# Windowed attention into a gated MLP on one core: stores of weight sums held until the last weight is decoded, and the product of a head pair issued together with the scores two pairs on

## The chip, the cores and the metric

The kernel runs on 1 core of one Trainium2 chip. The metric is the time of one execution in device microseconds (us). Before the change the median of 3 runs is 877.01 us (874.94 to 877.79).

## The reference

What is computed, cut to what matters: masked attention for 8 batches x 8 heads of 576 positions and 64 channels, and then a two-layer MLP on the 4608 tokens of 512 channels.

```python
scores = q @ k.T / sqrt(64)                       # per batch and head, 576 x 576
mask_plain = (rel >= 0) & (rel < 32)              # heads 0 to 3, rel = query - key
mask_dil = (rel >= 0) & (rel < 128) & (rel % 4 == 0)      # heads 4 to 7
attn = softmax(where(mask, scores, -1e9))
x = (attn @ v) -> [4608, 512]
h = x @ w_in                                      # w_in 512 x 2048
g = h * (1 / (1 + exp(-1.702 * h)))
out = g @ w_out                                   # w_out 2048 x 512, all float32
```

## The kernel before, in words

**Attention.** The work is cut into 32 entries `k`, each a pair of heads of one batch: batch `b = k // 4`, four entries a batch (`NC` is 4). For each entry TensorE makes `scores(k)` (L429, 72 small matmuls with q and k as 64 x 32 and 64 x 64 operands, into the tile `sp`); VectorE, ScalarE and GpSimd make the softmax (`softmax`, which starts with `exponentials`); the weights are transposed and copied into the one tile `bt`; TensorE makes `product(k)` (L537, 36 matmuls of 96 x 64, 32 of them into the tile `av` and 4 into a spare strip of an `sp` tile); ScalarE and VectorE take the result out (`drain_x`). For entries 0 to 7 (`masked`) the mask is added by a matmul; from entry 8 on VectorE adds it while it takes the scores out of `sp` (`add_mask`). For entries 4 to 7 the copies into `bt` are DMAs (L496), later they are done by ScalarE and VectorE. There is one buffer each of q/k (`qk`), v (`v`), `bt`, `av` and `sp`, and two each of the softmax tiles, taken by turns.

**The order of an entry's steps** is written in `attention(k)`. Before, `scores(k + 1)` is its own step on TensorE, issued by `alone(k + 1)`, and `product(k)` is another, which comes later.

**MLP.** Batches 0 to 2 go through groups `m0` to `m2` (`Group`): for each of 16 slices `f` of the hidden width, 12 matmuls into the one bank `hp_m` (L769), ScalarE's tanh (L777), VectorE's gating (L778), which frees `hp_m`, a split into a high and a low part (`gh`, `gl`), and then 12 matmuls into the accumulators `acc_m` (L678, L679, L682). Batches 3 to 7 and the rest go through three blocks `p`, `q`, `r` (`Block`), which multiply sums of tokens with sums of weights (seven products for eight). The blocks read the sums from DRAM: `sum_weights(u)`, u from 0 to 7, writes three of seven sums as they stand in the weights (L794, three stores of 256 KB, so 24 in all), makes the other four on VectorE and GpSimd in arena areas 0 to 7, and writes these (L815, 1 MB). The down-weights of slices 9 to 15 are also copied to DRAM (L996, seven stores of 512 KB to `outs`), since the blocks overwrite their places.

**Decoding.** The float32 weights come as 32 chunks of 512 KB (`wi` and `wo` by turns, chunk 2f is w_in of slice f and chunk 2f + 1 is w_out of it). `decode(n)` fetches a chunk into one of five cells (L332) and splits it into a high and a low part with some six steps on ScalarE (L342, L343, L336), VectorE (L346 and others) and GpSimd. Slice f of group m0 can be made only when chunk 2f is decoded, and added to the accumulators only when chunk 2f + 1 is. So m0 runs beside the decoding, and m1 and all that follows runs after it.

**What sets the order.** Nothing is issued as the loops run. Each step is given to a planner (`Plan.add`) with its costs by engine, an urgency (smaller first), the names it reads and writes. `Plan.ordered` then goes through time by these costs, puts each step on the engine on which it would end first, and writes out one fixed order for each engine; a step's place is given by

```python
when, e = min((min(start(i, e) for i in mine[e]), e) for e in range(5) if mine[e])
here = [i for i in mine[e] if start(i, e) <= when]
i = min(here, key=lambda i: ops[i][1])
```

that is, of the steps that can start, the one with the smallest urgency. The urgencies that matter here: pieces of `hp` and `acc` 0, decoding `25 + 2.3 n`, attention of entries 8 to 11 `2000 + c`, `sum_weights` `2500 + 10 u`, the stores to `outs` 2600; scores and products have 100000 less than their entry. All DMAs spoken of here are issued by one queue, SP's, in the order so found. Engines take their instructions strictly in that order.

Of the kernel before, what the change touches and what calls it, by code (L numbers as in the profile page):

```python
# [17 lines left out]
P = 128  # L18
NC = DM // P
NF = DF // P  # L20
# [150 lines left out]
def tile_windowed_attention_then_gated_mlp(  # L171
# [27 lines left out]
    def bank(shape, tag, name):  # L199
        return ps.tile(shape, F32, tag=tag, name=name)  # L200
# [159 lines left out]
    def lots(k):  # L360

        if 0 < k < NC:
            return f"first qk{k}", f"first v{k}"
        return "qk0", "v0"
# [75 lines left out]
    def exponentials(k, urgency):  # L440
        u, y = pairs[k], k % 2
        pr, mx = prs[y], mxs[y]
        PR, MX = f"pr{y}", f"mx{y}"
        held = ("sp",) if masked(k) else ()

        def sp():
            return u["all"] if masked(k) else pr

        if FIRST * NC <= k < INNER:
            add_mask(k, urgency)  # L450
        add({DVE: 0.80}, urgency, lambda e: V.tensor_reduce(out=mx, in_=sp(), axis=AX.X, op=ALU.max),
            held or (PR,), (MX,))
        add({DVE: 0.80}, urgency, lambda e: pair(
            e, pr, sp(), mx[:, :, :, None].broadcast_to([P, 2, QT, W]), ALU.subtract), (*held, MX), (PR,))
        add({ACT: 0.75}, urgency, lambda e: A.activation(prs[y], prs[y], AF.Exp, scale=0.125), (), (PR,))
# [68 lines left out]
    def product(k):  # L524
        u = pairs[k]
        if k < INNER:
            u["av"] = bank([P, GT], "av", f"av_{k}")
            sp = pairs[k + 1]["sp"] if k + 1 < INNER else bank([P, 2, GT], "sp", f"rest_{k}")
            u["rest"] = sp[:, 1, QT * W:QT * W + LT]
        else:  # L530
            sp = bank([P, 2, GT], "sp", f"av_{k}")
            u["av"], u["rest"] = sp[:, 0], sp[:, 1, 0:LT]
        for m in range(NW):
            for a in range(2):
                rows = slice(D * a, D * a + D)
                dst = u["av"][rows, D * m:D * m + D] if m < NW - 1 else u["rest"][rows]
                T.matmul(dst, u["v"][a][0:KW, m], bt[0:KW, a, m], start=True, stop=True, skip_group_check=True)  # L537
# [77 lines left out]
    def attention(k, urgency):  # L615

        def alone(j):
            add({PE: 1.6 if masked(j) else 1.1}, urgency - 1.0e5, lambda e: scores(j),
                (lots(j)[0], *(["mask"] if dilated(j) else [])), ("sp", "left", f"scores{j}"), 1.0)
            if j >= INNER:  # L620
                add_mask(j, urgency)

        if k in (NC, INNER):
            load_qk(k)
            alone(k)
        load_v(k)
        more = k + 1 < len(pairs) and k + 1 != INNER
        if more:
            load_qk(k + 1)
        softmax(k, urgency)  # L630
        if more:
            alone(k + 1)
        add({PE: 1.25}, urgency - 1.0e5, lambda e: product(k),
            (lots(k)[1], *(f"bt.{m}" for m in range(8)), *([f"scores{k + 1}"] if more else [])),
            ("sp",) if k >= INNER else ("left", "av"), 1.0)
        drain_x(k, urgency)


    def unit(i):
# [147 lines left out]
    def sum_weights(u):  # L787


        f, g = u, u + PAIRS  # L790
        urgency = 2500.0 + 10.0 * u
        half = slice(0, 2 * P), slice(2 * P, 4 * P)
        for n, (w, cols) in enumerate(((f, half[0]), (f, half[1]), (g, half[1]))):
            add({DMA: 262}, urgency, lambda e, n=n, w=w, cols=cols: load(  # L794
                sums[7 * u + n].rearrange("p (h n) -> p h n", h=2), f32(wi(w)[:, :, cols])), (f"wi{w}",), (f"sums{u}.{n}",))
        b1, b2 = arena[:, 6], arena[:, 7]
        t = area(4, 2).rearrange("p (i n) -> p i n", i=4)
        parts_ = area(0, 4).rearrange("p (h i n) -> p h i n", h=2, i=4)

        def both(e, dst, w):  # L800
            pair(e, dst, f32(wi(w)[:, 0]), f32(wi(w)[:, 1]), ALU.add)

        add(add_costs, urgency, lambda e: both(e, b1, f), (f"wi{f}",), own(6))
        add(add_costs, urgency, lambda e: both(e, b2, g), (f"wi{g}",), own(7))
        keys = (*own(4), *own(5))
        for dst, x, y, costs in ((0, lambda: b2[:, half[0]], lambda: b1[:, half[0]], 0), (2, lambda: b2[:, half[1]], lambda: b2[:, half[0]], 0),
                                 (1, lambda: b2[:, half[1]], lambda: t[:, 0], 0), (3, lambda: b1[:, half[1]], lambda: t[:, 1], 0)):
            add({DVE: -0.40, POOL: 0.75}, urgency, lambda e, dst=dst, x=x, y=y: pair(e, t[:, dst], x(), y(), ALU.subtract),
                ("A6", "A7"), keys)
        places = [k for i in range(4) for k in own(i)]  # L810
        high = parts_[:, 0].bitcast(F32R)
        add({ACT: 1.05, DVE: -0.75}, urgency, lambda e: copy(e, high, t), ("A4", "A5"), places)
        add({DVE: -1.25, POOL: 2.6}, urgency, lambda e: pair(e, parts_[:, 1].bitcast(F32R), t, parts_[:, 0], ALU.subtract),
            ("A4", "A5", "A0", "A1"), ("A2", "A3"))
        add({DMA: 1049}, urgency, lambda e: load(  # L815
            sums[7 * u + 3:7 * u + 7].rearrange("i p (h n) -> p h i n", h=2), parts_), [f"A{i}" for i in range(4)], [f"sums{u}.{n}" for n in range(3, 7)])
# [165 lines left out]
    for b, g in enumerate(main):  # L982
        g.split_x()
        if b == 0:
            for n in range(2, 2 * NF - 8):
                decode(n, 25.0 + 2.3 * n)
            zeroed = [f"bt.{m}" for m in range(8)]
            add({POOL: 1.2}, 20.0, lambda e: G.memset(bt[0:KW], 0.0), (), ("bt", "btl", *zeroed))
            add({ACT: 0.5}, 30.0, lambda e: mask_dilated(), (), ("mask",))
        if b == 1:  # L990
            for c in range(NC):
                attention(2 * NC + c, 2000.0 + c)
            for u in range(PAIRS):
                sum_weights(u)
            for f in range(KEPT, NF):
                add({DMA: 524}, 2600.0, lambda e, f=f: load(outs[f].rearrange("p (h n) -> p h n", h=2), f32(wo(f))),  # L996
                    (f"wo{f}",), (f"outs{f}",))
        if b == 2:
            for k in range(3 * NC, INNER):
                attention(k, 1000.0 * (k // NC) + k % NC)  # L1000
        for f in range(NF):
            g.up(f)
            if b == 0 and f == 2:
                for c in range(NC):
                    attention(NC + c, 46.0 + 12.9 * c)
                for n in range(2 * NF - 8, 2 * NF):
                    decode(n, 25.0 + 2.3 * n)
# [74 lines left out]
```

## Time and profile before

| | |
|---|---|
| median of 3 runs | 877.01 us |
| the profiled execution's own time | 877.82 us |
| its span, first to last instruction | 876.1 us |
| TensorE matmuls busy | 853.5 us (97%) |
| VectorE, ScalarE, GpSimd busy | 521.6, 450.8, 148.8 us |
| mean granted TensorE clock | 0.992 |
| moved by DMA | 145.81 MB |

PE is TensorE's matmuls, PEld its loading of weights, which overlaps them, DVE is VectorE, ACT is ScalarE, POOL is GpSimd, SP the queue that issues the DMAs. A row of a timeline reads: start, length, engine, line, operation, tiles and count, and in brackets the idle time of the engine before it and what ended that. A matmul's record is longer than the time it holds TensorE, since matmuls are pipelined: a stream of 128 x 512 matmuls starts one every 0.227 us (12 of them fill 2.72 us) though each record has 0.39 us. The chain of waits is followed back from the last instruction: at each step to what released it.

### The profile page before, as it was taken

To read this page: it belongs to the slowest core of one execution; us is meant where nothing else is said; L and a number is where in the kernel's file an instruction comes from. 1 tells how busy PE (TensorE), PEld (TensorE's weight loads), DVE (VectorE), ACT (ScalarE), POOL (GpSimd) and SP (SyncE) were. 2 spreads that over 40 slices of the span, in tenths; PEclk is the share of its full clock that TensorE was granted. 3 is DMA by queue.
4 is the path that set the end of the run, shared out by engine and by line. 5 is a ranking of instruction groups with operands and counts; after the bars stand their busy time and mean duration, and the time that the engine had idled before them with its cause. 6 is when DMAs were issued, how large, how long until landed. Compare 5 with 4: busy or idle time off the path is not lost.

```text
span 876.1 us, 17851 instructions
## 1 busy us (share of the span) xinstructions
PE 853.5 (97%) x7160; PEld 688.8 (79%) x7160; DVE 521.6 (60%) x923; ACT 450.8 (51%) x789; POOL 148.8 (17%) x156
## 2 busy tenths in 40 slices
PE   6999989999999999999999999999999999999997
PEld 3677767878877877778788888888888888888786
DVE  6797877788577677777744544534346433434321
ACT  7897866656354555666753434433334343333322
POOL 3351414664111251021200100000001000000000
PEclk9799999999999999999999999999999999999999
DMA  9697884756364404977754631455456045543221
GB/s 351 188 348 225 248 296 161 221 177 196 108 207 151 130 29 122 325 227 241 232 176 128 215 99 48 146 151 168 124 142 220 1 136 143 153 145 108 48 73 49
DMA packets 89011, 145.81 MB, mean 166 GB/s; under 512 B 25952, under 2 KB 40544, under 8 KB 88928
## 3 DMA queue, kind: packets, MB, share of 16 engines
q1 hardware_dynamic: 88784, 144.54, 52.3%
q8 instruction: 57, 0.93, 0.4%
q14 instruction: 26, 0.21, 0.1%
q10 hardware_dynamic: 144, 0.13, 0.0%
HBM read 109.25 MB, written 34.08 MB: 164 GB/s over the span
## 4 chain that ended last, share of the span: by engine, by line
PE 88%; DMA 7%; DVE 2%; ACT 2%; issue 1%; SPq 0%; DVEq 0%; ACTq 0%
PE hp_m L769 13%; PE up_r L877 9%; PE up_p L877 8%; PE up_q L877 8%; PE acc_m L678 4%; PE acc_m L682 4%; PE acc_m L679 4%; PE av L537 3%; PE sp L429 3%; DMA qk<-qk_dram 2%; DMA arena<-wi_dram 2%; PE acc_pa L678 2%; PE acc_pa L682 2%; PE acc_rb L678 2%; PE acc_pa L679 2%; PE acc_rb L682 2%
## 5 line engine op out<-in xcount | busy, mean ns | idle before, releaser
L769 PE MATMUL hp_m<-xs,wi_kept 128*128 128x512 f32 x504 | 129.1, 399 | 4.1 <-DVE arena L778 3.6
L769 PEld LDWEIGHTS hp_m<-xs,wi_kept 128*128 128x128 f32 x504 | 93.6, 190 | 26.2 <-DVE arena L778 5.3
L297 DVE TENSOR_TENSOR gl<-arena,gh 128x512 fp32r<-128x512 f32 x108 | 78.8, 730 | 48.8 <-ACT gh L290 23.6
L290 ACT ACTIVATE gh<-arena 128x512 fp32r<-128x512 f32 x109 | 68.9, 632 | 56.3 <-DVE arena L909 15.8
L877 PE MATMUL up_p<-wi_kept,xs 128*128 128x512 f32 x336 | 86.8, 394 | 0.0
L877 PE MATMUL up_r<-wi_kept,xs 128*128 128x512 f32 x336 | 83.3, 390 | 0.0
L877 PE MATMUL up_q<-wi_kept,xs 128*128 128x512 f32 x336 | 83.3, 390 | 0.0
L297 POOL TENSOR_TENSOR pr<-pr,sm 128x320 f32<-128x320 f32 x64 | 51.7, 825 | 153.4 <-DVE sm L461 138.7
L908 ACT ACTIVATE arena<-arena 128x512 f32<-128x512 f32 x57 | 36.0, 632 | 80.3 <-DVE arena L297 80.2
L877 PEld LDWEIGHTS up_q<-wi_kept,xs 128*128 128x128 f32 x336 | 63.1, 188 | 13.0
L877 PEld LDWEIGHTS up_r<-wi_kept,xs 128*128 128x128 f32 x336 | 63.1, 188 | 13.0
L877 PEld LDWEIGHTS up_p<-wi_kept,xs 128*128 128x128 f32 x336 | 62.4, 188 | 13.4
L290 ACT ACTIVATE bt<-ct 32x320 f32<-32x320 f32 x125 | 58.7, 470 | 10.3 <-DVE ct L482 7.8
L678 PE MATMUL acc_m<-gh,wo_kept 128*128 128x512 f32 x156 | 62.5, 400 | 0.0
L679 PE MATMUL acc_m<-gh,wo_kept 128*128 128x512 f32 x156 | 60.9, 390 | 0.0
L909 DVE SCALAR_TENSOR_TENSOR arena<-arena 128x512 f32<-128x512 f32 x57 | 41.3, 724 | 25.1 <-ACT arena L908 25.0
L297 POOL TENSOR_TENSOR arena<-arena 128x256 f32<-128x256 f32 (+2 forms) x43 | 40.2, 947 | 57.4 <-DVE arena L297 24.4
L297 POOL TENSOR_TENSOR wi_kept<-arena,wi_kept 128x512 fp32r<-128x512 f32 x14 | 19.9, 1423 | 172.4 <-PE up_q L877 102.1
L777 ACT ACTIVATE arena<-hp_m 128x512 f32<-128x512 f32 x48 | 28.9, 601 | 34.2 <-PE hp_m L769 34.0
L778 DVE SCALAR_TENSOR_TENSOR arena<-arena,hp_m 128x512 f32<-128x512 f32 x48 | 32.9, 686 | 18.8 <-ACT arena L777 18.5
L682 PE MATMUL acc_m<-gl,wo_kept 128*128 128x512 f32 x156 | 42.5, 393 | 0.0
L297 DVE TENSOR_TENSOR arena<-up_q,arena 128x512 f32<-128x512 f32 x19 | 13.1, 689 | 49.2 <-PE up_q L877 49.1
(194 smaller groups left out, 1687.7 us busy)
## 6 DMA issues: line engine op xcount, KB each, us to landing
xs<-sums SPq DMA_DIRECT2D x168, 256.0 KB, 2.7
qk<-qk_dram SPq DMA_DIRECT2D x29, 576.0 KB, 5.0
v<-vp_dram SPq DMA_DIRECT2D x56, 216.0 KB, 3.0
wo_kept<-outs SPq DMA_DIRECT2D x18, 512.0 KB, 3.5
out_dram<-arena SPq DMA_DIRECT2D x35, 256.0 KB, 2.7
sums<-arena SPq DMA_DIRECT2D x8, 1024.0 KB, 5.6
arena<-wi_dram SPq DMA_DIRECT2D x15, 512.0 KB, 5.7
arena<-wo_dram SPq DMA_DIRECT2D x15, 512.0 KB, 6.3
```

The source lines that it names most:

```text
L290: A.activation(dst, src, AF.Copy, scale=scale)
L297: (V if e == DVE else G).tensor_tensor(out=dst, in0=a, in1=b, op=op)
L429: T.matmul(dst[:, w:w + n], u["qk"][rows, at:at + 32], u["qk"][rows, S + first:S + first + n], start=not masked(k), stop=True, tile_positi ...
L678: T.matmul(self.acc[j], w[:, 0, cols], high, start=f == self.order[0], stop=False)
L679: T.matmul(self.acc[j], w[:, 1, cols], high, start=False, stop=False)
L682: T.matmul(self.acc[j], w[:, 0, P * j:P * j + P], low, start=False, stop=f == self.order[-1])
L769: T.matmul(hps[f], wi(f)[:, st, cols], mv[:, c], start=c == 0 and k == 0, stop=c == NC - 1 and k == 2)
L777: add({ACT: 0.60}, -10.0, lambda e: A.activation(g32, hps[f], AF.Tanh, scale=0.851), (place,), ("g32",))
L778: add({DVE: 0.69}, -10.0, lambda e: V.scalar_tensor_tensor(out=g32, in0=g32, scalar=1.0, in1=hps[f], op0=ALU.add, op1=ALU.mult), (place,), ...
L877: T.matmul(self.banks[place], xs[:, slot, at:at + P], wi_kept[:, 2 * a + c, mv], start=fresh and c == 0 and k == 0, stop=c == 1 and k == 2 ...
L908: add({ACT: 0.60}, -10.0, lambda e: A.activation(unit(tmp), src(), AF.Tanh, scale=0.851), need, own(tmp))
L909: add({DVE: 0.70}, -10.0, lambda e: V.scalar_tensor_tensor(out=unit(dst), in0=unit(tmp), scalar=1.0, in1=src(), op0=ALU.add, op1=ALU.mult) ...
```

## The change

It has two parts.

**Stores held back.** Each `sum_weights(u)` step that stores a sum as it stands (24 stores of 256 KB), the step that makes the first inner sum, and each store to `outs` (7 of 512 KB) now also reads the name `wo15`, the last chunk. So none of them can be ordered before the last chunk is decoded. (The inner sums could not be made before either, since their areas 6 and 7 hold the decoder's words.)

**Product and scores joined.** A new `following(k)` says which entry's scores go with entry k: `k + 2` for entries 8 to 19 (batches 2 to 4), else `k + 1`, and none past the end of a stretch (entries 18, 19 and 31 have none). For k from 8 to 17 scores(k + 2) and product(k) become one step on TensorE, scores first, so that the two stand next to each other; 10 such steps are made. Scores 9 is made by itself ahead of softmax 8. `add_mask` moves from the softmax to just behind the scores.

```diff
-        if FIRST * NC <= k < INNER:
-            add_mask(k, urgency)
...
-            sp = pairs[k + 1]["sp"] if k + 1 < INNER else bank([P, 2, GT], "sp", f"rest_{k}")
+            n = following(k)
+            sp = pairs[n]["sp"] if n else bank([P, 2, GT], "sp", f"rest_{k}")
...
-            if j >= INNER:
+            if not masked(j):
                 add_mask(j, urgency)
 
+        n = following(k)
         if k in (NC, INNER):
             load_qk(k)
             alone(k)
         load_v(k)
-        more = k + 1 < len(pairs) and k + 1 != INNER
-        if more:
-            load_qk(k + 1)
+        if n and n > k + 1:
+            if k == FIRST * NC:
+                load_qk(k + 1)
+                alone(k + 1)
+            load_qk(n)
+        elif n:
+            load_qk(n)
         softmax(k, urgency)
-        if more:
-            alone(k + 1)
-        add({PE: 1.25}, urgency - 1.0e5, lambda e: product(k),
-            (lots(k)[1], *(f"bt.{m}" for m in range(8)), *([f"scores{k + 1}"] if more else [])),
-            ("sp",) if k >= INNER else ("left", "av"), 1.0)
+        joint = n == k + 2
+        if n and not joint:
+            alone(n)
+
+        def work(e):
+            if joint:
+                scores(n)
+            product(k)
+
+        need = [lots(n)[0] if joint else f"scores{n}"] if n else []
+        places = ("sp",) if k >= INNER else ("left", "av", "sp") if joint else ("left", "av")
+        add({PE: 2.2 if joint else 1.25}, urgency - 1.0e5, work,
+            (lots(k)[1], *(f"bt.{m}" for m in range(8)), *need), places, 1.0)
+        if joint:
+            add_mask(n, urgency)
         drain_x(k, urgency)
+
+    def following(k):
+
+        n = k + 2 if FIRST * NC <= k < INNER else k + 1
+        return n if n < (INNER if k < INNER else len(pairs)) else None
...
+        decoded = f"wo{NF - 1}"
...
-                sums[7 * u + n].rearrange("p (h n) -> p h n", h=2), f32(wi(w)[:, :, cols])), (f"wi{w}",), (f"sums{u}.{n}",))
+                sums[7 * u + n].rearrange("p (h n) -> p h n", h=2), f32(wi(w)[:, :, cols])), (f"wi{w}", decoded), (f"sums{u}.{n}",))
...
-        add(add_costs, urgency, lambda e: both(e, b1, f), (f"wi{f}",), own(6))
+        add(add_costs, urgency, lambda e: both(e, b1, f), (f"wi{f}", decoded), own(6))
...
-                    (f"wo{f}",), (f"outs{f}",))
+                    (f"wo{f}", f"wo{NF - 1}"), (f"outs{f}",))
```

The planner then finds another order on every engine. Three places of it follow.

SP's queue near the end of the decoding, before. L332 fetches a chunk to be decoded, L794 stores a sum of weights, L996 stores a down-weight to `outs`, L394 and L376 load v and q/k of an entry:

```order
L332 DMA arena<-wo_dram 128x512
L332 DMA arena<-wi_dram 128x512
L794 DMA sums<-wi_kept 256x1x256
L332 DMA arena<-wo_dram 128x512
L996 DMA outs<-wo_kept 128x1024
L794 DMA sums<-wi_kept 256x1x256
L332 DMA arena<-wi_dram 128x512
L394 DMA v_1496<-vp_dram 96x576 x2
L996 DMA outs<-wo_kept 128x1024
L332 DMA arena<-wo_dram 128x512
```

The last row there is the fetch of the last chunk. The same stretch of SP's queue now, up to the fetch of the last chunk and a little past it (L494 copies into `bt`, which was L496):

```order
L332 DMA arena<-wi_dram 128x512
L494 DMA bt<-ct_88 32x10x32 x8
L332 DMA arena<-wo_dram 128x512
L332 DMA arena<-wi_dram 128x512
L332 DMA arena<-wo_dram 128x512
L394 DMA v_1520<-vp_dram 96x576 x2
L494 DMA bt<-ct_89 32x10x32 x6
```

The stores L794 and L996 have left the stretch of the fetches altogether; ahead of the last fetch stood 21 of L794 and 4 of L996 before, and none now. They stand together behind it, as SP's queue shows now, from the first held store on (L814 is L794 before, L1016 is L996, L722 stores m0's result):

```order
L814 DMA sums<-wi_kept 256x1x256 x20
L814 DMA sums<-wi_last 256x1x256
L814 DMA sums<-wi_kept 256x1x256
L722 DMA out_dram<-arena 128x512 x2
L814 DMA sums<-wi_kept 256x1x256
L814 DMA sums<-wi_last 256x1x256
L722 DMA out_dram<-arena 128x512
L1016 DMA outs<-wo_kept 128x1024
L722 DMA out_dram<-arena 128x512
L1016 DMA outs<-wo_kept 128x1024 x3
L1016 DMA outs<-wo_last 128x1024 x3
L394 DMA v_1977<-vp_dram 96x576 x2
```

The last row is the load of v for entry 9, and behind it comes q/k of entry 11: both are queued behind all the held stores.

TensorE in group m1, around a product of an entry in batch 2, before (L429 scores, L537 product, L769 `hp`, L678, L679 and L682 `acc`):

```order
L537 MATMUL av_2186<-bt,v_2038 64x64 x16
L537 MATMUL sp_2063<-bt,v_2038 64x64 x2
L769 MATMUL hp_m_5_2180<-xs,wi_kept 128x512 x9
L678 MATMUL acc_m_0_1889<-gh_73,wo_kept 128x512
L679 MATMUL acc_m_0_1889<-gh_73,wo_kept 128x512
L678 MATMUL acc_m_1_1894<-gh_73,wo_kept 128x512
L679 MATMUL acc_m_1_1894<-gh_73,wo_kept 128x512
L678 MATMUL acc_m_2_1917<-gh_73,wo_kept 128x512
L679 MATMUL acc_m_2_1917<-gh_73,wo_kept 128x512
L429 MATMUL sp_2237<-qk_2107 32x64 x36
```

TensorE in group m1 now, at the second joined step, that of product 9 and scores 11 (L536 product, L697, L698 and L701 `acc`, the other lines as above):

```order
L698 MATMUL acc_m_2_1892<-gh_73,wo_kept 128x512
L429 MATMUL sp_2112<-qk_1982 32x64 x36
L536 MATMUL av_2149<-bt,v_1977 64x64 x16
L536 MATMUL sp_2112<-bt,v_1977 64x64 x2
L697 MATMUL acc_m_3_1898<-gh_73,wo_kept 128x512
L698 MATMUL acc_m_3_1898<-gh_73,wo_kept 128x512
L701 MATMUL acc_m_0_1880<-gl_75,wo_kept 128x512
```

Two visits to small matmuls with MLP work between them have become one visit, and the product's spare strip now lies in the `sp` tile of the entry two on.

## The prediction

> **What bounds the kernel now.** First the page's sums, then busy time by stage.
>
> ```profile
> span 876.1 us, 17851 instructions
> PE 853.5 (97%) x7160; PEld 688.8 (79%) x7160; DVE 521.6 (60%) x923; ACT 450.8 (51%) x789; POOL 148.8 (17%) x156
> ```
>
> ```profile
> 60.00:100.00 40.00, 37.55 (x359) 29.58 (x358) 32.83 (x60) 32.82 (x53) 14.18 (x12) 1.00 0.77 242
> 100.00:128.00 28.00, 23.52 (x198) 18.46 (x197) 21.67 (x41) 20.33 (x35) 6.67 (x5) 1.00 0.92 295
> 300.00:355.00 55.00, 55.00 (x666) 43.78 (x665) 42.92 (x85) 30.30 (x57) 18.13 (x17) 1.00 0.37 111
> 500.00:655.00 155.00, 155.00 (x686) 128.47 (x685) 66.84 (x101) 58.00 (x97) 1.77 (x1) 1.00 0.43 128
> ```
>
> Columns: stretch, its length, busy PE, PEld, DVE, ACT, POOL, granted clock, DMA share, GB/s. TensorE sets the time: from 128 us on it never waits (55.00 of 55, 155.00 of 155), so there only less work on TensorE shortens the kernel. Between 60 and 128 us it loses 40.00 - 37.55 + 28.00 - 23.52 = 6.9 us, and DMA runs at 0.77 and 0.92. So two questions decide: which of these waits go, and what TensorE saves by the joined steps. The timeline of TensorE shows each wait:
>
> ```profile
> 82.88 3.02 PE L769 MATMUL hp_m<-xs,wi_kept 128*128 128x512 f32 x12 [1.28 <-DVE arena L778]
> 89.80 2.33 PE L769 MATMUL hp_m<-xs,wi_kept 128*128 128x512 f32 x9 [1.17 <-DVE arena L778]
> 98.19 2.90 PE L769 MATMUL hp_m<-xs,wi_kept 128*128 128x512 f32 x12
> 107.88 1.40 PE L537 MATMUL av<-bt,v 96*64 96x64 f32 x32 [0.45 <-DMA bt<-ct]
> 119.18 3.02 PE L769 MATMUL hp_m<-xs,wi_kept 128*128 128x512 f32 x12 [1.18 <-DVE arena L778]
> 127.74 4.62 PE L769 MATMUL hp_m<-xs,wi_last 128*128 128x512 f32 x12 [2.82 <-DVE arena L778]
> 128.00:135.00 7.00, 7.00 (x34) 5.32 (x35) 5.69 (x11) 4.08 (x7) 1.67 (x1) 0.76 0.44 157
> ```
>
> Four waits are for L778, the gating that frees the one bank `hp_m`. What made it late stands on ScalarE and, in the chain of waits, behind that:
>
> ```profile
> 80.96 0.67 ACT L343 ACTIVATE arena<-arena 128x512 uint32<-128x512 uint32 x1 [3.54 <-DMA arena<-wi_dram]
> 124.10 0.67 ACT L343 ACTIVATE arena<-arena 128x512 uint32<-128x512 uint32 x1 [2.84 <-DMA arena<-wo_dram]
> 126.29 0.68 ACT L777 ACTIVATE arena<-hp_m 128x512 f32<-128x512 f32 x1
> ```
>
> ```profile
> 73.75 7.19 DMA arena<-wi_dram
> 114.75 9.33 DMA arena<-wo_dram
> ```
>
> ScalarE stands in its fixed order at a decode step (L343) whose chunk has not landed; the tanh (L777) that TensorE needs is queued behind it. These chunks took 7.19 and 9.33 us from issue to landing. Around the start of both, stores were in the queue:
>
> ```profile
> 71.71 1.95 SPq L794 DMA_DIRECT2D sums<-wi_kept  x3
> 112.93 0.34 SPq L996 DMA_DIRECT2D outs<-wo_kept  x1
> ```
>
> **Part 1: stores held back.** What there is to win: gaps of 1.28 + 1.17 + 0.45 + 1.18 + 2.82 = 6.9 us. A gap counts from the modelled end of the last matmul (records of 0.39 us, one started every 0.227 us), so each wait costs 0.16 more: 0.8. The last wait is followed by a clock of 0.76, and 12 matmuls take 4.62 us where 2.90 is usual: 1.7. The first matmul after a wait costs 3.02 - 2.90 twice: about 0.3 with the av row. In all 9.7 us, which is the most that part 1 can give.
>
> How much of it comes back? DMA first:
>
> ```profile
> DMA packets 14453, 16.22 MB, mean 280 GB/s; under 512 B 8623, under 2 KB 11183, under 8 KB 14447
> sums<-wi_kept SPq DMA_DIRECT2D x10, 256.0 KB, 6.7
> outs<-wo_kept SPq DMA_DIRECT2D x4, 512.0 KB, 8.2
> outs<-wo_last SPq DMA_DIRECT2D x1, 512.0 KB, 6.8
> 70.00:128.00 58.00, 51.07 (x512) 39.77 (x511) 45.33 (x84) 43.71 (x72) 14.97 (x12) 1.00 0.88 280
> 110.00:120.00 10.00, 8.82 (x107) 6.77 (x106) 7.41 (x15) 7.15 (x16) 0.10 (x1) 1.00 1.02 365
> ```
>
> The first three rows are the DMA view of 70 to 128 us: 10 x 0.262 + 5 x 0.524 = 5.2 of 16.2 MB are these stores. At the 365 GB/s of a full stretch they are 14 us of 58 x 0.88 = 51 us. Without them DMA needs 37 of 58 us and is not the limit. VectorE is then: its 45.33 us of work here are the same. How densely can it be packed, in its fixed order?
>
> ```profile
> 20.00:60.00 40.00, 36.00 (x584) 27.16 (x584) 34.75 (x63) 35.31 (x55) 15.96 (x14) 0.87 0.81 276
> 60.00:70.00 10.00, 10.00 (x46) 8.27 (x45) 9.17 (x17) 9.43 (x15) 5.89 (x5) 1.00 0.58 170
> ```
>
> At the 0.82 of 60 to 100 us (32.83 of 40) the 45.33 us take 55.3 us, 2.7 us less than 58; at the 0.87 of 20 to 60 us 52.1, or 5.9 less; at the 0.917 of 60 to 70 us 49.4, or 8.6 less. I take 0.88, close to the middle row, since slices and chunks are still tied to each other in fixed orders: 45.33 / 0.88 = 51.5, **6.5 us less**. Bounds: 2.7 and 9.7.
>
> The added wait: SP's stores wait for the last chunk, and no work stands still for that, but v of entry 9 and q/k of entry 11 are queued behind them (a rival, below). The sums are first needed by block p:
>
> ```profile
> 350.83 4.33 DMA xs<-sums
> ```
>
> That is over 200 us later; their 24 x 0.262 + 7 x 0.524 = 10.0 MB are hidden in stretches with a DMA share like 0.37, so moving them costs nothing there. The inner sums keep their time, since they could not start before either.
>
> **Part 2: joined steps.** One visit of each kind, warm and without a wait:
>
> ```profile
> 331.61 0.39 PE L679 MATMUL acc_m<-gh,wo_kept 128*128 128x512 f32 x1
> 331.93 0.97 PE L429 MATMUL sp<-qk 64*32 64x64 f32 x72
> 332.83 0.50 PE L678 MATMUL acc_m<-gh,wo_kept 128*128 128x512 f32 x1
> 333.17 0.40 PE L679 MATMUL acc_m<-gh,wo_kept 128*128 128x512 f32 x1
> 336.25 1.27 PE L537 MATMUL av<-bt,v 96*64 96x64 f32 x36
> 337.45 1.43 PE L769 MATMUL hp_m<-xs,wi_kept 128*128 128x512 f32 x5
> ```
>
> By starts: going in costs 331.93 - 331.61 - 0.23 = 0.09 us, the scores and the way out hold TensorE 0.90, and the first large matmul after them takes 333.17 - 332.83 = 0.34 instead of 0.23, that is 0.11. A product is 337.45 - 336.25 = 1.20 with the same edges. Apart: 0.20 + 0.90 + 0.20 + 1.20 = 2.50. Joined: 0.20 + 0.90 + 1.20 = 2.30, if the switch from scores to product costs what the switch out of scores does (it is inside the 0.90). So 0.20 us a pair, and 10 pairs: **2.0 us**, all on the path, since TensorE does not wait there. No warm row shows scores directly ahead of a product. If that switch also cost 0.11 like the return to large matmuls, 0.1 is left, 1.0 in all; if it cost nothing, at most 0.1 more is won, 3.0 in all. The Trainium skill (TensorEngine Tiling (Array Packing), Key Properties) says that a change of the tiling mode drains TensorE; by that the joined step still pays for its inner switch and the sum is the 2.0, and 3.0 is excluded.
>
> VectorE's `add_mask` is the same work in another place. What hides the longer distance from scores to product is that softmax tiles are double and TensorE has other work; if that fails, see the fourth rival.
>
> **The sum.** Profiled execution 877.82 (span 876.1 and 1.7 around it) - 6.5 - 2.0 = 869.3 us. It lies 0.8 above the median of the three runs, so for the median: 877.0 - 8.5 = **868.5 us**.
>
> **Rivals.**
>
> *All waits go.* TensorE catches up with the decoder nowhere, and the inner switch is free: 877.0 - 9.7 - 3.0 = 864.3. Against it: the new order has the decoder as tight to the slices as the old. Chance 0.10.
>
> *The decoder's engines were the bound all along.* ScalarE and VectorE have 9.43 and 9.17 of 10 us at 60 to 70 us, where DMA has only 0.58. Then part 1 gives nothing and part 2 its 2.0: 875.0. Against it: the waits of 3.54 and 2.84 us above are for DMA. Chance 0.11.
>
> *The held stores block the loads behind them (slower).* Place: product 9 with scores 11, behind five and a half rounds of hp and acc of m1. A round is 5.5 us by the first two rows here, so 5 x 5.5 + 2.3 for the first joined step + 2.7 + 1.4 = 33.9 us after slice 0 of m1 starts.
>
> ```profile
> 143.07 2.90 PE L769 MATMUL hp_m<-xs,wi_kept 128*128 128x512 f32 x12
> 148.60 2.92 PE L769 MATMUL hp_m<-xs,wi_kept 128*128 128x512 f32 x12
> 134.37 0.68 DVE L297 TENSOR_TENSOR wo_last<-arena,wo_last 128x512 fp32r<-128x512 f32 x1
> 100.00:110.00 10.00, 9.53 (x72) 7.69 (x71) 9.27 (x18) 8.25 (x14) 3.00 (x3) 1.00 0.85 227
> ```
>
> The last chunk is decoded at 135.05, slice 0 of m1 starts at 143.07; both move by 6.5. The queue then holds 10.0 MB of stores, 1.05 MB of m0's result, 0.44 of v and 0.59 of q/k, 12.0 MB, and has 143.07 - 135.05 + 33.9 = 41.9 us. With 3 us for landing it needs 12.0 / 38.9 = 308 GB/s; below that TensorE waits. At the 227 GB/s of 100 to 110 us it takes 53 + 3 us: a wait of 14.1 us and 1.7 for the clock, 868.5 + 15.8 = 884.3. It outweighs the gain below 12.0 / (38.9 + 6.8) = 263 GB/s. Against it: the 365 GB/s above, in a stretch with such stores. [...] Chance 0.07.
>
> *The joined steps wait.* Scores and product now start at the later of two readinesses. The softmax of an entry must be through while one other joined step runs; if each of the 10 waits 0.7 us, as much as one step of VectorE, 868.5 + 7 = 875.5. Against it: no wait from 128 to 355 us before, with one entry less in flight. Chance 0.06.
>
> **The numbers.** My case has the remaining 0.66. Its own range comes from the bounds: from 864.3 to 877.0 - 2.7 - 1.0 = 873.3. With the first rival inside it and the 0.8 between runs at the upper end: 864.0 to 874.0, which leaves out the last three rivals and a little. A difference of 0.3%, 2.6 us, is about what a measurement of this kernel can tell from none. Faster by that: my case, the first rival and a few hundredths of the others, 0.80; the same: the second and fourth, 0.13; slower: the third, 0.07.
>
> **What would show it.** Right: the chunks land in 3 to 6 us, ScalarE's waits at L343 shrink, slice 0 of m1 starts at about 136.5 instead of 143.07, and the ten joined visits take 2.3 us each from large matmul to large matmul, with no gap on TensorE up to 830 us. Wrong: a gap at the second joined step that ends with a load of v or q/k (third rival); waits at L778 of the old length with DMA idle (second); short gaps ahead of most joined steps, ended by copies into `bt` (fourth).

## The result and the profile after

| | before | after |
|---|---|---|
| median of 4 runs each | 876.74 us (874.94 to 877.79) | 866.61 us (866.24 to 867.56) |
| profiled execution | 877.82 us | 866.49 us |
| its span | 876.1 us | 864.8 us |
| TensorE matmuls busy | 853.5 us (97%) | 847.6 us (98%) |
| slice 0 of m1 starts | 143.07 us | 132.93 us |
| block q starts | 500.13 us | 490.06 us |

The kernel after takes 0.9888 of the time before, 95% interval 0.987 to 0.9907: it is faster by 10.1 us. The forecast was 8.5 us faster, 868.5 us, with a range of 864.0 to 874.0. In two later sets of runs, on two chips, the same pair differs by 8.5 and 10.2 us. Two runs far above the others of their kernel are left out of every median: one of before at 2147.48 us, and one at 1192.39 us with a granted clock of 0.72, of the kernel with half the bytes, whose only trace is of that run.

The last two rows of the table in the timelines of TensorE after, and block q before (slice 0 of m1 before stands in the prediction):

```profile
132.93 2.89 PE L788 MATMUL hp_m<-xs,wi_kept 128*128 128x512 f32 x12
490.06 1.52 PE L897 MATMUL up_q<-wi_kept,xs 128*128 128x512 f32 x6
```

```profile
500.13 1.52 PE L877 MATMUL up_q<-wi_kept,xs 128*128 128x512 f32 x6
```

The windows of the profile after, in the stretches that were shown of before (the columns are as there):

```profile
20.00:60.00 40.00, 35.92 (x586) 27.07 (x586) 35.13 (x65) 35.21 (x55) 15.96 (x14) 0.87 0.62 200
60.00:100.00 40.00, 40.00 (x373) 32.20 (x372) 36.36 (x62) 36.26 (x59) 13.82 (x12) 1.00 0.72 218
100.00:128.00 28.00, 28.00 (x318) 22.34 (x317) 26.59 (x45) 22.40 (x41) 10.31 (x8) 1.00 0.57 155
70.00:128.00 58.00, 58.00 (x645) 46.25 (x644) 54.05 (x93) 49.75 (x85) 18.90 (x16) 1.00 0.70 208
128.00:160.00 32.00, 32.00 (x239) 26.27 (x239) 25.17 (x43) 18.93 (x35) 18.32 (x19) 1.00 1.00 353
```

TensorE now fills 60 to 128 us whole, 40.00 of 40 and 28.00 of 28, where it lost 6.9 us. VectorE does 54.05 us of work in the 58 us in which it did 45.33, and DMA falls from 0.88 to 0.70. The stores stand in the last row: DMA at 1.00 of its share and 353 GB/s, and TensorE is full all the same.

The fetches from 70 to 128 us (size, median time from issue to landing), first before:

```profile
arena<-wo_dram SPq DMA_DIRECT2D x7, 512.0 KB, 6.3
arena<-wi_dram SPq DMA_DIRECT2D x6, 512.0 KB, 7.5
```

The same stretch after, with the one store in it, and the waits of ScalarE for a chunk at L343 after:

```profile
arena<-wo_dram SPq DMA_DIRECT2D x6, 512.0 KB, 4.6
arena<-wi_dram SPq DMA_DIRECT2D x5, 512.0 KB, 4.4
sums<-wi_kept SPq DMA_DIRECT2D x1, 256.0 KB, 5.5
```

```profile
ACT arena L343 <- DMA arena<-wo_dram: 0.9, 1, 0.9
ACT arena L343 <- DMA arena<-wi_dram: 0.5, 1, 0.5
```

The chunks land in 4.4 to 4.6 us (medians), where they had taken 6.3 and 7.5, and the two that mattered 7.19 and 9.33; ScalarE waits 0.9 and 0.5 us for them at L343 between 60 and 128 us, where one wait alone had 3.54.

What did not come as forecast stands later in the span. These are the waits of TensorE for L797 (which is L778 of before) in the whole span, the timeline of TensorE at the two places, and that of ScalarE ahead of the first:

```profile
PE hp_m L788 <- DVE arena L797: 1.7, 2, 1.1
```

```profile
230.06 3.05 PE L788 MATMUL hp_m<-xs,wi_last 128*128 128x512 f32 x12 [1.13 <-DVE arena L797]
...
286.88 0.96 PE L788 MATMUL hp_m<-xs,wi_kept 128*128 128x512 f32 x3 [0.56 <-DVE arena L797]
```

```profile
226.62 1.06 ACT L290 ACTIVATE arena<-arena 128x1024 fp32r<-128x1024 f32 x1 [3.98 <-DMA sums<-arena]
227.71 0.95 ACT L290 ACTIVATE bt<-ct 32x320 f32<-32x320 f32 x2
228.68 0.60 ACT L796 ACTIVATE arena<-hp_m 128x512 f32<-128x512 f32 x1
```

ScalarE stands 3.98 us at a copy into areas that a 1 MB store (L835, `sums<-arena`, the made sums) still reads; the tanh L796 that TensorE needs is queued behind it. SP's queue shows what the store was issued with, and the chain of waits how long it took:

```profile
216.36 0.80 SPq L394 DMA_DIRECT2D v<-vp_dram  x2
217.25 0.37 SPq L376 DMA_DIRECT2D qk<-qk_dram  x1
```

```profile
217.67 8.87 DMA sums<-arena
```

v and q/k of an entry leave SP within 1.3 us ahead of the store: one joined step, behind which the next matmul starts at 216.25 us, sets the places of both free. The store lands after 8.87 us. So part 2 brought a wait of the same kind as those that part 1 took away: a transfer that lands late, ScalarE in fixed order at it, the tanh behind.

### The profile page after: what moved, and what is told of

The parts are those of the page before. It is cut to its first block, busy times and chain, and to the rows that moved or that the text cites. A ratio compares the mean times of both kernels' runs of the same rounds, so it can differ in the third digit from the quotient of the medians.

```text
span 864.8 us, 17828 instructions
## 1 busy us (share of the span) xinstructions
PE 847.6 (98%) x7160; PEld 687.6 (80%) x7160; DVE 521.3 (60%) x899; ACT 458.0 (53%) x812; POOL 148.4 (17%) x157
## 4 chain that ended last, share of the span: by engine, by line
PE 92%; DMA 4%; DVE 1%; ACT 1%; issue 1%; SPq 0%; ACTq 0%
PE hp_m L788 14%; PE up_r L897 9%; PE up_q L897 9%; PE up_p L897 8%; PE acc_m L701 5%; PE acc_m L697 5%; PE acc_m L698 4%; PE av L536 3%; PE sp L429 3%; PE acc_pa L697 2%; DMA sums<-arena 2%; PE acc_rb L697 2%; PE acc_pa L701 2%; PE acc_pa L698 2%; PE acc_rb L698 2%; PE acc_rb L701 2%
## 5 line engine op out<-in xcount | busy, mean ns | idle before, releaser
L788 PE MATMUL hp_m<-xs,wi_kept 128*128 128x512 f32 x504 | 127.0, 396 | 1.0 <-DVE arena L797 0.6
L290 ACT ACTIVATE gh<-arena 128x512 fp32r<-128x512 f32 x112 | 70.8, 632 | 53.6 <-DVE arena L929 15.6
L297 POOL TENSOR_TENSOR pr<-pr,sm 128x320 f32<-128x320 f32 x64 | 49.4, 792 | 137.9 <-DVE sm L459 130.7
L290 ACT ACTIVATE bt<-ct 32x320 f32<-32x320 f32 x137 | 64.3, 469 | 12.0 <-DVE ct L480 9.2
L697 PE MATMUL acc_m<-gh,wo_kept 128*128 128x512 f32 x156 | 61.5, 394 | 0.0
L698 PE MATMUL acc_m<-gh,wo_kept 128*128 128x512 f32 x156 | 60.8, 390 | 0.0
L297 POOL TENSOR_TENSOR arena<-arena 128x256 f32<-128x256 f32 (+2 forms) x44 | 42.6, 980 | 65.8 <-DVE arena L297 29.9
L796 ACT ACTIVATE arena<-hp_m 128x512 f32<-128x512 f32 x48 | 28.7, 598 | 40.4 <-PE hp_m L788 37.1
L297 POOL TENSOR_TENSOR wi_kept<-arena,wi_kept 128x512 fp32r<-128x512 f32 x12 | 17.0, 1416 | 187.9 <-PE up_q L897 102.1
L701 PE MATMUL acc_m<-gl,wo_kept 128*128 128x512 f32 x156 | 43.4, 396 | 0.0
L297 DVE TENSOR_TENSOR arena<-up_r,arena 128x512 f32<-128x512 f32 x19 | 13.1, 689 | 49.2 <-PE up_r L897 49.1
```

Of the source, the lines that this page charges most:

```text
L290: A.activation(dst, src, AF.Copy, scale=scale)
L297: (V if e == DVE else G).tensor_tensor(out=dst, in0=a, in1=b, op=op)
L697: T.matmul(self.acc[j], w[:, 0, cols], high, start=f == self.order[0], stop=False)
L698: T.matmul(self.acc[j], w[:, 1, cols], high, start=False, stop=False)
L701: T.matmul(self.acc[j], w[:, 0, P * j:P * j + P], low, start=False, stop=f == self.order[-1])
L788: T.matmul(hps[f], wi(f)[:, st, cols], mv[:, c], start=c == 0 and k == 0, stop=c == NC - 1 and k == 2)
```

## The experiments

The runs were made on three chips, and each time stands beside runs of the kernel before on the same chip. Its median is 874.82 us on the first (each part alone, the joining left out, an eighth of the bytes), 875.07 on the second (half the bytes, the matmul put between, the other queue, after once more) and 876.0 on the third (the small store, the store in halves, after and part 1 alone once more). Ratios are to the runs of before on the same chip, with a 95% interval.

### One part at a time

**Part 1 alone**: of the diff, only `decoded` and `wo{NF - 1}` in the reads of the stores and of the first inner sum.

> Part 1 alone: the stores held until the last chunk is decoded, attention as before the change. Main theory (the head's gain is all part 1): slice 0 of m1 starts at 132.9 us as in the changed kernel, against 143.1 before. Of the whole time two theories differ: if part 2 is worth its 2.0 us, this kernel takes 866.6 + 2.0 = 868.6 us; if part 2's 2.0 us are eaten by the two new waits of TensorE at 229 and 286 us, it takes 866.6 us, and these two waits are not there.

Measured: 867.82 us, ratio 0.9921 [0.9903, 0.9938]. Slice 0 of m1 starts at 133.23 us, as after (132.93), behind one wait of 0.84: the head's gain is part 1's. The two waits near 229 and 286 us are not there. The time lies between the two that were expected.

**Part 2 alone**: the stores, and the first inner sum, read no `decoded` any more.

```diff
-  f32(wi(w)[:, :, cols])), (f"wi{w}", decoded), (f"sums{u}.{n}",))
+  f32(wi(w)[:, :, cols])), (f"wi{w}",), (f"sums{u}.{n}",))
...
-  (f"wo{f}", f"wo{NF - 1}"), (f"outs{f}",))
+  (f"wo{f}",), (f"outs{f}",))
```

> Part 2 alone: joined steps, the stores not held. Head as before: waits of 6 to 7 us between 60 and 128 us, slice 0 of m1 at 142 to 143 us. If part 2 is worth 2.0 us: 876.7 - 2.0 = 874.7 us. If nothing is left of it because the joined order makes waits of its own: 876.7 us, with new waits of 1 to 2 us between 130 and 350 us.

Measured: 878.67 us, ratio 1.0037 [1.002, 1.0054]. Part 2 alone is slower, by 3.9 us, against both values expected. Its head has waits of 4.5 us where before's has 6.9 (slice 0 of m1 at 141.96 us); the largest loss behind it stands on ScalarE and TensorE at 210 to 224 us of its trace, and in the window from 216 to 224 us:

```profile
215.38 1.06 ACT L290 ACTIVATE arena<-arena 128x1024 fp32r<-128x1024 f32 x1 [4.28 <-DMA sums<-arena]
216.35 0.58 ACT L796 ACTIVATE arena<-hp_m 128x512 f32<-128x512 f32 x1
```

```profile
218.81 4.60 PE L788 MATMUL hp_m<-xs,wi_kept 128*128 128x512 f32 x12 [2.31 <-DVE arena L797]
```

```profile
216.00:224.00 8.00, 5.69 (x19) 4.20 (x18) 4.16 (x4) 6.48 (x14) 4.24 (x5) 0.79 0.51 176
```

It is the same kind of wait as in the kernel after, 2.31 us of it, and the granted clock is 0.79 in the stretch that holds the wait and the matmuls behind it, where 12 matmuls take 4.60 us for 2.89. From slice 0 of m1 to the first matmul of block q this trace has 359.70 us and before's 357.06, 2.64 more. By terms: -2.0 for the visits, 2.31 + 0.16 for the wait (0.16 as in the prediction), 1.7 for the slow matmuls, 0.17 + 0.16 for a small wait at 189.8 us, and 0.5 for a wait for q/k near 368 us that is longer than before's (0.76 against 0.24) make +3.0. The rest of the 3.9 us is not accounted for: the traced run of before, at 877.82 us, stands 3.0 above the median on this chip, so its head is no measure for these runs.

**The order two on without the joining**: scores(k + 2) is a step by itself.

```diff
-        joint = n == k + 2
-        if n and not joint:
+        joint = False
+        if n:
             alone(n)
```

> The changed kernel with scores(k + 2) as a step of its own, still issued two entries ahead, so that TensorE visits small matmuls 10 times more often. By the price of a visit read from starts (0.20 us each) TensorE's work grows by 2.0 us: 866.6 + 2.0 = 868.6 us where no wait changes. If the inner switch of a joined step costs as much as a visit, no difference. If the two waits at 229 and 286 us come from the joining, they go and the time is 866.6 us; if they come from the held sums, they stay.

Measured: 867.61 us, ratio 0.9921 [0.9901, 0.994], like part 1 alone, and between the two values expected. TensorE has no wait from 60 to 356 us, not even near 230 us. The loads of v and q/k now leave SP 3.2 us apart (at 214.84 and 218.03 us), and the 1 MB store, issued at 219.71, lands after 5.1 us instead of 8.87. So the wait near 230 us belongs to the joining, neither to the held stores nor to the greater distance: all six traces with joined steps and whole 1 MB stores have such a wait between 218 and 232 us (0.59 to 2.31 us), and the three traces with held stores and no joining have none there. ScalarE's waits for these stores are not the joining's alone: they are 4.0 us in before and 6.5 in part 1 alone, against 10.9 after, but spread over smaller waits, of which the longest is 2.7 us.

### Part 1: bytes or queue

The stores could have hurt through their bytes or through their place in SP's queue. In the next two kernels the order of before is kept on every engine, and only the sizes change: the stores of the sums as they stand and of the down-weights write 16, or 64, of their 128 partitions, and the blocks read other sums in their place.

```diff
-  sums[7 * u + n].rearrange("p (h n) -> p h n", h=2), f32(wi(w)[:, :, cols])), ...
+  sums[7 * u + n][0:P // 8].rearrange("p (h n) -> p h n", h=2), f32(wi(w)[0:P // 8, :, cols])), ...
...
-  load(outs[f].rearrange("p (h n) -> p h n", h=2), f32(wo(f))),
+  load(outs[f][0:P // 8].rearrange("p (h n) -> p h n", h=2), f32(wo(f)[0:P // 8])),
```

An eighth of the bytes:

> The kernel before, with its order of instructions on every engine and every wait as it was, but each of the 31 stores of weight sums and down-weights writes only an eighth of its bytes (16 partitions of 128; the blocks then read other sums in their place, so the product is not the reference's). Theory A, bandwidth (the stores' bytes stand in front of the chunks in the DMA engines): the waits of 6.9 us at hp go, slice 0 of m1 at 133 to 135 us, whole time 867 to 869 us. Theory B, queue (SP stands at a store whose weights are not decoded yet and issues the next fetch late): nothing changes, 143 us and 876.7 us.

Measured: 867.79 us, ratio 0.9915 [0.9894, 0.9937], as part 1 alone. The windows of its trace, the row of a store in the DMA view (now 32 KB), and slice 0 of m1 in the timeline of TensorE:

```profile
60.00:100.00 40.00, 40.00 (x373) 32.19 (x372) 34.98 (x64) 35.74 (x57) 14.88 (x13) 1.00 0.73 213
100.00:128.00 28.00, 28.00 (x251) 22.59 (x250) 25.72 (x49) 23.12 (x43) 8.94 (x7) 1.00 0.62 182
```

```profile
sums<-wi_kept SPq DMA_DIRECT2D x9, 32.0 KB, 4.9
```

```profile
131.79 2.89 PE L769 MATMUL hp_m<-xs,wi_kept 128*128 128x512 f32 x12
```

All the head's waits are gone with the stores still in their old places in the queue, and slice 0 of m1 starts even earlier than forecast (1.4 of the 11.3 us lie ahead of 56 us, in the start of the run). SP takes as long to issue the small stores as the large ones (three L794 in 1.84 us, before in 1.95), so the time of issuing is not the cause either. It was the size of the stores: their bytes, and with them their packets, which shrink by the same factor and were not told apart.

Half of the bytes:

> As the run with an eighth of the stores' bytes, with one half: the kernel before, same order and waits, the 31 stores write 64 of 128 partitions (the blocks read other sums in their place, not the reference's product). If bytes in the DMA engines are the cause and the loss grows evenly with them, about half of the 10 us remains: slice 0 of m1 at 138 us, 872 us. If DMA only has to stay below VectorE's pace, nearly all is won at a half already: 133 to 135 us, 867 to 869 us.

Measured: 870.1 us (median of four), ratio 0.9933 [0.991, 0.9957]: 4.9 us less than before, where an eighth brought 7.0 on another chip. That lies between the two values expected; it fits the bytes, though the intervals overlap, and no trace shows where the rest is lost.

### Part 2: what a joined visit costs

A joined visit in the kernel after, timeline of TensorE:

```profile
254.37 0.39 PE L698 MATMUL acc_m<-gh,wo_kept 128*128 128x512 f32 x1
254.68 0.97 PE L429 MATMUL sp<-qk 64*32 64x64 f32 x72
255.58 1.15 PE L536 MATMUL av<-bt,v 96*64 96x64 f32 x32
256.56 0.29 PE L536 MATMUL sp<-bt,v 96*64 96x64 f32 x4
256.78 0.50 PE L697 MATMUL acc_m<-gh,wo_kept 128*128 128x512 f32 x1
257.12 0.40 PE L698 MATMUL acc_m<-gh,wo_kept 128*128 128x512 f32 x1
```

Counted as in the prediction: 254.68 - 254.37 - 0.23 = 0.08 going in, 256.78 - 254.68 = 2.10, and 257.12 - 256.78 - 0.23 = 0.11 coming out, 2.29 us in all; forecast 2.30. The ten joined visits hold TensorE for 2.09 to 2.14 us from their first scores to the next large matmul. In the experiment, one 128 x 512 matmul is put between the scores and the product, its result overwritten, so that the joined step has the switches of two visits again:

```diff
-            product(k)
+                product(k, True)
...
+        if between:
+            T.matmul(u["av"], wi_kept[:, 13, 0, 0:P], wi_kept[:, 13, 0, 0:GT], start=True, stop=True)
```

> The changed kernel with one large matmul of 128 x 512 put between scores and product of each of the 10 joined steps (its result is overwritten); order otherwise the same. If a visit to small matmuls costs 0.20 us and the joined step saves one, 10 x (0.23 + 0.20) = 4.3 us more, 870.9 us. If a visit costs nothing (the saving of the joined step was no more than a place in the order), 2.3 us more, 868.9 us.

Measured: 870.91 us, ratio 0.9938 [0.9917, 0.9958], 4.3 us above the kernel after on the same chip. Four of its six runs lie at 870.9 to 871.0 us, but two at 868.6 and 868.8, where the other theory had it, so the time alone does not decide. The visit in its trace does:

```profile
257.02 0.97 PE L429 MATMUL sp<-qk 64*32 64x64 f32 x72
257.92 0.50 PE L533 MATMUL av<-wi_kept 128*128 128x512 f32 x1
258.35 1.15 PE L538 MATMUL av<-bt,v 96*64 96x64 f32 x32
```

From the first scores to the first product are 258.35 - 257.02 = 1.33 us, after 255.58 - 254.68 = 0.90. Of the 0.43 more, 0.23 are the matmul itself, and 0.20 the switches: the price of a visit is 0.20 us, as forecast. All ten visits of that trace have 1.33 or 1.34 us there.

### The new wait near 230 us

The store `sums<-arena` could land late because of its place in SP's queue, behind the loads of v and q/k; because of its bytes beside theirs; or the engines could be full there whatever it does.

**The made sums stored from ScalarE's queue**, the order otherwise the same:

```diff
-        add({DMA: 1049}, urgency, lambda e: load(
+        add({DMA: 1049}, urgency, lambda e: nc.scalar.dma_start(
```

> The changed kernel with the eight 1 MB stores of made sums issued from ScalarE's queue instead of SP's; the order of everything else is the same. Theory Q (the wait at 229 us comes from a store that stands in SP's queue behind a load of v, which waits for the joined step): that wait goes, TensorE gains 1.3 us there, 865.3 us, if ScalarE's own waits at the eight stores delay no tanh. Rival (ScalarE and VectorE are simply full there): the wait stays at 229 us, 866.6 us or more. The wait at 286 us has another cause in both and stays.

and the kernel after beside it:

> The changed kernel once more, beside the next three on the same chip: 0.988 to 0.990 of the kernel before. Its waits at 229 us (1.1 us) and 286 us (0.6 us) show again if they belong to the order and not to one run.

Measured: 867.39 us, ratio 0.9909 [0.9885, 0.9933], and 866.61 us, ratio 0.9891 [0.9869, 0.9914], for the kernel after. From ScalarE's queue:

```profile
218.38 0.60 ACTq L835 DMA_DIRECT2D sums<-arena  x1
222.05 0.60 ACT L796 ACTIVATE arena<-hp_m 128x512 f32<-128x512 f32 x1 [4.09 <-PE hp_m L788]
222.58 0.74 ACT L453 ACTIVATE pr<-pr 128x640 f32<-128x640 f32 x1
223.40 0.63 ACT L290 ACTIVATE gh<-arena 128x512 fp32r<-128x512 f32 x1
227.64 1.06 ACT L290 ACTIVATE arena<-arena 128x1024 fp32r<-128x1024 f32 x1 [3.60 <-DMA sums<-arena]
```

```profile
231.08 3.07 PE L788 MATMUL hp_m<-xs,wi_last 128*128 128x512 f32 x12 [0.75 <-DVE arena L797]
```

Issued by another queue at 218.38, the store still holds ScalarE until 227.64, and TensorE still waits 0.75 us, against 0.81 in the kernel after on this chip. SP's order falls as the cause. The wait near 286 us is in neither of these two traces, so it does not belong to the order alone; the kernel after has instead a wait of 0.55 us for q/k at 244.82 us.

**An eighth of the bytes of that store**, order as after:

```diff
-  sums[7 * u + 3:7 * u + 7].rearrange("i p (h n) -> p h i n", h=2), parts_), ...
+  sums[7 * u + 3:7 * u + 7, 0:P // 8].rearrange("i p (h n) -> p h i n", h=2), parts_[0:P // 8]), ...
```

> The kernel after in the same order of instructions; only the stores of the sums that are made (1 MB each, L835) write 16 of 128 partitions, and the blocks read another sum in their place, so their products are not the reference's. Theory R: the wait of about 1.3 us at hp near 230 us comes from such a store, which lands some 9 us late because it meets the loads of v and q/k that a joined step sets free at once, while ScalarE's next copy into the same areas, and the tanh behind it, stand in line. Then ScalarE's wait for sums<-arena (near 4 us) and TensorE's wait near 230 us both go, and the time is 1.0 to 1.5 us below the kernel after of this call. Rival: ScalarE and VectorE are full there whatever the store does; then the wait stays and the time is that of the kernel after, within 0.4 us.

with the kernel after and part 1 alone on the same chip:

> The kernel after once more, beside part 1 alone on the same chip: 866.6 us, give or take 0.6. The first joined visit at 2.30 us and a wait of 0.8 to 1.3 us near 230 us in its trace.

> Part 1 alone once more, beside the kernel after. By the terms read from the traces (10 joined visits save 2.0 us, the waits that came with them cost 1.1 to 2.0) it is 0 to 1 us above the kernel after; if the joined steps brought their 2.0 whole, it is 2 us above.

Measured: 864.36 us (ratio 0.9859 [0.9834, 0.9884]) against 865.84 us (0.9881 [0.9856, 0.9906]) for the kernel after, which is itself 0.2 below the least that was expected of it; the small store brings 1.5 us (their runs just overlap: 862.26 to 865.0, and 864.47 to 866.93). It is 867.62 us (0.9905 [0.9882, 0.9927]) for part 1 alone. ScalarE and TensorE with the small store:

```profile
222.39 1.05 ACT L290 ACTIVATE arena<-arena 128x1024 fp32r<-128x1024 f32 x1
```

```profile
227.67 1.10 PE L701 MATMUL acc_m<-gl,wo_last 128*128 128x512 f32 x4
228.61 2.95 PE L788 MATMUL hp_m<-xs,wi_last 128*128 128x512 f32 x12
```

No bracket on either: the wait for the store and the wait near 230 us are both gone, while there is one of 0.61 near 285 us, as in the first trace of after. The size of the 1 MB store makes the wait. That it meets the loads set free by the joined step is read from SP's rows and from the kernel without the joining, where the same store lands after 5.1 us and there is no such wait; those loads were not shrunk by themselves.

The kernel after and part 1 alone on this chip give part 2 its price: the kernel after is 1.8 us below part 1 alone, and their runs do not overlap (864.47 to 866.93, and 867.12 to 869.45). The expectation had 0 to 1 us, or 2 us if the joined steps brought all; it is nearer to the second. Part 1 alone had waits of its own of 0.53 us at 212 us and 0.20 near 488 us in this run, and the kernel after one of 0.68 near 230 us, less than the 0.8 expected, and one of 0.44 for q/k near 355 us, so their traces differ by little besides the visits: from slice 0 of m1 to block q 358.26 against 356.39 us, 1.9 less.

**A version from this**: the store cut into two halves of 512 KB, the first issued as soon as it is made, ScalarE's next copy made to wait for that half alone.

```diff
-  places = [k for i in range(4) for k in own(i)]
+  places = [[k for i in (2 * h, 2 * h + 1) for k in own(i)] for h in range(2)]
...
+        for h in range(2):
+            add({DMA: 524}, urgency, lambda e, h=h: load(
+                sums[7 * u + 3:7 * u + 7, :, 2 * P * h:2 * P * h + 2 * P].rearrange("i p n -> p i n"), parts_[:, h]), ...
```

> The kernel after with each 1 MB store of made sums cut into two of 512 KB, the first issued as soon as its half is made, and ScalarE's next copy made to wait for that half alone. Theory R: the wait of about 1.3 us near 230 us goes or shrinks below 0.5 us, and the time is 0.8 to 1.5 us below the kernel after of this call. Rival (the engines are full there, or the new order moves the wait elsewhere): within 0.5 us of the kernel after, or slower.

Measured: 864.86 us, ratio 0.9869 [0.9843, 0.9895], 1.0 us below the kernel after. The waits of TensorE in 132 to 356 us of its trace, and the place near 230 us:

```profile
PE hp_m L788 <- DVE arena L797: 0.5, 1, 0.5
```

```profile
227.43 1.10 PE L701 MATMUL acc_m<-gl,wo_last 128*128 128x512 f32 x4
228.37 2.95 PE L788 MATMUL hp_m<-xs,wi_last 128*128 128x512 f32 x12
```

The wait near 230 us is gone; 0.5 us stand at another place (175 us). This version is faster than the kernel before, but not shown to be faster than the kernel after, since the runs of the two overlap (863.16 to 866.99, and 864.47 to 866.93).

## Why the prediction was right, and where it was off

**The bound (right).** TensorE sets the time, and the loss in the head was ScalarE standing at a late chunk with the tanh behind it. Before's order with an eighth of the stores' bytes loses all the head's waits, so the stores' size was the cause, as part 1's working had it. The rival that the decoder's engines were the bound falls with that: there they did the same work in the same order, and TensorE had no wait from 60 to 350 us. That TensorE never waits from 128 us on was read from two stretches and is nearly so: before has waits of 0.24 us near 364 us and 0.59 near 828 us, the second also after, so the sign "no gap on TensorE up to 830 us" could hardly have come true.

**Part 1 (right in kind, too small).** Forecast: slice 0 of m1 6.5 us earlier, bounds 2.7 and 9.7. In the profiled pair it came 143.07 - 132.93 = 10.1 us earlier; some 0.3 of that lies ahead of 60 us, in the start of the run, and the rest is the whole of the 9.7. The mis-sized term is VectorE packed at 0.88. It was taken from rows of before, where VectorE itself had waited for late transfers. With the chunks in time it reached 54.05 / 58 = 0.93, and it drew in work of the attention as well, while no slice of TensorE was late; with before's own order and the small stores it has 52.26 / 58 = 0.90, and TensorE no wait there. Its density of before was a result of the waits and no limit on taking them away. By the medians part 1 alone gives 7.0 and 8.4 us on two chips, less than the profiled pair: the profiled execution of before stands 3.0 above the 874.82 of the first of them. So the term was short by 0.5 to 1.9 us in the medians, by 3.3 in the profiled pair. The range, which went to the rival that all waits go, had room for it.

**Part 2 (term right, sum short of a wait).** 0.20 us a visit is confirmed twice, by the rows and by the matmul put between. The Trainium skill (TensorEngine Tiling (Array Packing), Key Properties) has a change of tiling mode drain TensorE; the rows agree, as from scores to product 0.90 us pass in the joined visit, no less than from scores to a large matmul, and 3.0 us was excluded rightly. But "all on the path, since TensorE does not wait there" did not hold: in the profiled pair slice 0 of m1 to block q took 357.06 us before and 357.13 after, since the two waits cost 1.13 + 0.56 and twice 0.16, 2.0 us, and a wait for q/k near 356 us is 0.3 longer than before's. The fourth rival had a price for waits, but looked for them ahead of the joined steps, for copies into `bt`; they came at `hp`, by way of ScalarE and a store. The question left out was which transfers a joined step starts together. The waits vary from run to run (1.13, 0.8 and 0.68 us near 230 us in three traces; the one near 286 us is in the first of them alone), and on the third chip part 2 kept 1.8 of its 2.0.

**The sum (near, in part by luck).** In the first profiled pair part 1 brought 9.8 us for the 6.5 forecast, and part 2 nothing for its 2.0. The two errors pull in opposite directions, so that the sum came within 1.7 us (10.1, 8.5 and 10.2 us in the three sets of runs, for 8.5) does not mean that its terms did.

**The held stores (rival fell).** The second joined step was put 33.9 us behind slice 0 of m1, and starts so:

```profile
166.77 0.97 PE L429 MATMUL sp<-qk 64*32 64x64 f32 x72
```

166.77 - 132.93 = 33.8 us, with no wait. 308 GB/s was needed; 353 was moved from 128 to 160 us. The margin is small: with the made sums issued from ScalarE's queue, the same step starts behind a wait of 0.87 us for q/k, the very sign that the prediction had named for this rival.

**What stays open.** Part 1 alone takes 357.99 and 358.26 us from slice 0 of m1 to block q, before 357.06: 0.2 and 0.5 us of that are not in the waits of its traces. Its wait of 0.53 us at 212 us comes some 9 us after ScalarE had stood 2.22 us for a store of made sums, so a wait of this kind may also arise without the joining; that was not followed up. The wait of 0.6 us near 286 us, where VectorE stands for a load of tokens, was not tried.

## What to carry to other kernels

A density of an engine read from a stretch in which it waits tells how long it waited, not how densely it can work: bound the gain by TensorE's lost time, and lean to that bound if the thing that made it wait is taken away whole, as it was here. Where two steps become one, list every transfer that the new step sets free at once, and look for the store that has to land among them and for who stands behind it. A gain on the path and a new wait of the same size can hide each other: run each part alone.

## What the runs showed of the hardware

A wait of 2.31 us on TensorE (part 2 alone) was followed by a granted clock of 0.70 from 220 to 224 us, as 2.82 us had been before (0.76 from 128 to 135 us); after one of 1.13 us 12 matmuls took 3.05 us, hardly more than 2.89. In the head of part 2 alone, waits of 1.57 and 0.58 us with a single matmul between them came with 0.60 from 126 to 130 us. The Trainium skill (TensorE: Matmul & The Clock Gate, What's actually happening) puts the fall of the clock after an idle window of about 3.4 us; here shorter waits did it, so that the measured rows decide. So these waits of over 2 us cost more than their length: in part 2 alone 2.31 us of wait and 1.7 us of slow matmuls behind it.

Another queue made the 1 MB store no quicker: issued by ScalarE's at 218.38 us it held the next copy until 227.64, issued by SP's at 217.67 it landed after 8.87 us.
